# Retention, a gated product and an expert layer on one core: sums of weight quarters ordered anew, four tiles down at once in the blocks of sums, routing tile by tile

## The chip, the core and the metric

One core of a Trainium2 chip runs the program. A core has five engines, each with an instruction stream of its own that runs strictly in order: TensorE (PE in the profile; PEld is its weight load), VectorE (DVE), ScalarE (ACT), GpSimd (POOL), and SyncE (SP), which here issues most DMAs. Engines wait for one another through semaphores. The metric is device time in microseconds (us), lower is better.

## The reference

Inputs are drawn at random; 3072 tokens (4 sequences of 768) have 512 features. Three layers follow one another:

```
state = gamma * state + k v^T ; y = scale * q state          # per head, 64x64 state
a = x @ w_a ; b = x @ w_b ; x2 = (a * b) @ w_out             # 512 -> 1536 -> 512
e = argmax(x2 @ w_gate) ; out = p_e * sigmoid(x2 @ w_output_gate)[e] * relu(x2 @ w1[e]) @ w2[e]
```

The expert layer has 8 experts; each token goes to one of them. Every large product is made of three matmuls (`mm3`): high by high, high by low, low by high, of numbers split into a rounded part and a rest.

## The kernel before, in words

Tokens run in four blocks, of 512, 512, 1024 and 1024. A tile is 128 tokens; a block of 1024 has eight. The index f runs over 12 groups of 128 of the 1536 middle features; each f needs a slice of `w_a`, `w_b` and `w_out`.

**Blocks 0 and 1** are done plainly: per f two projections (`proj`, 12 matmuls each), the gate, and `down` for four tiles (12 matmuls). Block 0 also decodes the weights. Between its products, block 1 runs four other lines of work: the attention of block 2 (`attention_steps`), the routing of block 0's tiles, the weight sums (`sum_steps`), and the preparation of block 2's inputs (`x_steps`).

**The weight sums.** Blocks 2 and 3 use a scheme of seven products of quarters in place of eight; it needs four sums of quarters of each weight slice. `sum_steps` has three steps for each f: load the slice (`wsum<-wab_d`, SP), four adds on POOL (L626), split on ACT and DVE (L631, L632) and store to `q_d` on SP (L633). They stand one f after another: load, adds, split and store, then the next f's load.

**Blocks 2 and 3** (`block_of_sums`): per f seven products of 6 matmuls each into three PSUM banks (p0, p1, acc3), adds of them on DVE, and `down` for three tiles (`NOW = 3`) of the f before. The gated values of the other five tiles are kept (`later`) and go down in deferred passes over all f: block 2 has one of five tiles, block 3 one of three ("3a") and one of two ("3b"). A deferred pass loads `w_out` slices again (`load_wo`, two ahead), splits them (ACT L545, POOL L546) and splits the kept values (`gd`, ACT L746, DVE L747).

**Routing.** Tiles 0 to 15 route on DVE: per tile eight ops of two inputs each (`junkd`, L367), one for each expert's column of `w_gate`, then some fifteen small ones, a gather of the chosen column of the second gate (POOL, L376) and its use (L398), and a scatter of the token's row into a table (POOL, L355). They go in groups of up to five tiles, two columns at a time; the columns are loaded for each group (`wcol`). Tiles 16 to 23 route on PE. The first expert starts on tokens whose routing is done: `TAIL` tells how many tokens at the end are left out of its first two gathers.

What sets the order of all this is the order of calls in Python: `spread` runs the steps of the lines at the calls of `slot()`, evenly between a first and a last slot given for each line. Each engine then keeps that order.

Of the kernel before, what the change touches and what calls it, by code (L numbers as in the profile page):

```python
# [7 lines left out]
F32 = mybir.dt.float32  # L8
# [8 lines left out]
T = B * S  # L17
# [21 lines left out]
NOW = 3  # L39
LATER = 640  # L40
TAIL = 640

NDVE = 16

ROUTE_FROM = [0, 4, 4, 0]
# [4 lines left out]
Q_POOL, V_POOL = {1, 2, 3, 4, 5, 6, 7}, {1, 2, 3, 4, 5, 6, 7}  # L50
# [6 lines left out]
def attention_moe_moe2(ctx: ExitStack, tc: tile.TileContext, a: dict, out: bass.AP):  # L57
# [241 lines left out]
    def route_steps(i):  # L299
# [11 lines left out]
        def s_l():  # L311
# [12 lines left out]
            oh = p2.tile([128, 8], BF16, tag="oh", name="oh")  # L324
# [37 lines left out]
        def s_d(wc, e0):  # L362
            if e0 == 0:
                st["lg"] = p1.tile([128, 8], F32, tag=f"lg{i % 5}", name="lg")
            for e in range(2):
                junk = lp(1).tile([128, 512], BF16, tag="junkd", name="junkd")
                dve.scalar_tensor_tensor(junk, x2t[i], 1.0, wc[:, e], op0=ALU.mult, op1=ALU.mult, accum_out=st["lg"][:, e0 + e : e0 + e + 1])  # L367

        def s_m():
# [15 lines left out]
            oh = p2.tile([128, 8], BF16, tag="oh", name="oh")  # L385
# [9 lines left out]
        def s_o():  # L395
            og = p2.tile([128, 1], F32, tag="og", name="og")
            junk = lp(1).tile([128, 512], BF16, tag="junkd", name="junkd")
            dve.scalar_tensor_tensor(junk, x2t.pop(i), 1.0, st.pop("wx"), op0=ALU.mult, op1=ALU.mult, accum_out=og)  # L398
# [9 lines left out]
        if i < NDVE:  # L408
            return [s_d, s_m, s_o, s_r]
        return [s_t, s_l, s_r]  # L410

    def route_order(rs):
        plain = [st for r in rs if len(r) == 3 for st in r]
        rs = [r for r in rs if len(r) > 3]
        if not rs:
            return plain
        out = []
        for e0 in range(0, E, 2):
            w = []

            def s_w(w=w, e0=e0):
                w.append(lp(2).tile([128, 2, 512], F32, tag="wraw", name="wcol"))
                sync.dma_start(w[0].rearrange("p e n -> p (e n)"), bass.AP(a["wgt"].tensor, a["wgt"].offset + e0 * DM, [[0, 128], [1, 2 * DM]]))

            cols.append(s_w)
            for r in rs:
                out.append(lambda r=r, w=w, e0=e0: r[0](w[0], e0))
            out.append(next_cols)
        next_cols()
        next_cols()  # L430
        out += [rs[0][1], lambda: None]
        for t, r in enumerate(rs):
            if t + 1 < len(rs):
                out += [lambda r=r, n=rs[t + 1]: (r[2](), n[1]()), r[3]]
            else:
                out += [r[2], r[3]]
        return out + plain

    cols = []

    def next_cols():
        if cols:
            cols.pop(0)()

# [86 lines left out]
    passes = [(j, f) for j in (1, 2, "2d", 3, "3a", "3b") for f in range(NF1)]  # L531
# [63 lines left out]
    def evac_x2(tok0, tiles, on_dve=()):  # L595
        for t in tiles:
            x2 = lp(6).tile([128, 512], F32, tag="x2", name="x2")
            if t in on_dve:
                dve.tensor_copy(x2, accs[t])
            else:  # L600
                act.copy(x2, accs[t])
            r0 = tok0 + 128 * t
            x2t[r0 // 128] = x2
            sync.dma_start(x2_d[r0 : r0 + 128, :], x2)
# [11 lines left out]
    def sum_steps(f, pair):  # L616
        st = {}

        def s_load():
            st["w"] = room(pair[0], [128, 8, 256], F32, "wsum")  # L620
            sync.dma_start(st["w"][:, :4].rearrange("p (a q) n -> p a (q n)", a=2), wab_d[f])

        def s_add():
            w = st["w"]
            for out, x, y, op in ((5, 2, 3, ALU.add), (4, 5, 0, ALU.subtract), (6, 0, 2, ALU.subtract), (7, 1, 4, ALU.subtract)):
                pool.tensor_tensor(w[:, out], w[:, x], w[:, y], op=op)  # L626

        def s_split():
            w = st.pop("w")[:, 4:]
            t = room(pair[1], [128, 4, 2, 256], F32R, "qsum")  # L630
            act.copy(t[:, :, 0], w)  # L631
# [676 lines left out]
```

## Time and profile before

| | us |
|---|---|
| three runs | 1161.74, 1163.3 (median), 1164.52 |
| profiled execution | 1167.32 |
| its span | 1165.6 |
| PE busy in it | 1022.1 (88%) |
| DVE busy | 642.7 (55%) |
| ACT, POOL busy | 407.8, 329.8 |

The span is from the first to the last instruction. The profiled execution is some 4 us above the median, so a change is best counted as a difference. The mean granted clock of TensorE was 0.931 of its higher level. Block 1 lies between about 142 and 359 us of the span, block 2 between 359 and 526, its deferred pass up to 598.4, block 3 up to 755.5, its two passes up to 845; the rest is the experts.

### The profile page before, as it was taken

Reading aid. Unit: us, or ns where it says so; the run is one execution under the profiler, and the core shown is the slowest. Engines: PE = TensorE matmul, PEld = TensorE weight load, DVE = VectorE, ACT = ScalarE, POOL = GpSimd, SP = SyncE. Lnnn points to the kernel's source line nnn. Section 1 sums busy time; section 2 is a strip of 40 time slices with the busy share of each in tenths; the row PEclk is TensorE's granted clock in tenths of the full one; section 3 lists DMA queues with packets and bytes.
Section 4 is the critical chain, followed back from the end, with each engine's and each line's share of the span. In section 5 each row is a group of like instructions: output and inputs, shape, how many; then the busy total and the mean of one; then the engine's idle time right before and its main releaser. Section 6 shows DMA issues by size and latency. Waiting matters only on the chain.

```text
span 1165.6 us, 19944 instructions
## 1 busy us (share of the span) xinstructions
PE 1022.1 (88%) x7287; PEld 828.2 (71%) x7288; DVE 642.7 (55%) x1444; ACT 407.8 (35%) x792; POOL 329.8 (28%) x299
## 2 busy tenths in 40 slices
PE   7999997765468999997869999877799999999997
PEld 5788885544346777775647877655589998888886
DVE  5899765353355665647945654444536544444551
ACT  3667622111123222223421222244435444334441
POOL 3221044444343111243431213344212122112211
PEclk8899998786688999998898999998799999999999
DMA  6999677566647666444274656434326555345530
GB/s 250 333 327 310 222 267 240 194 213 226 205 166 256 215 223 235 170 101 162 64 219 170 205 174 176 140 127 145 100 54 203 179 177 167 123 148 180 179 108 26
DMA packets 74520, 214.99 MB, mean 184 GB/s; under 512 B 12925, under 2 KB 22397, under 8 KB 69760
## 3 DMA queue, kind: packets, MB, share of 16 engines
q1 hardware_dynamic: 67104, 193.72, 50.1%
q0 software_dynamic: 6704, 18.93, 5.2%
q8 instruction: 82, 1.34, 0.5%
q10 hardware_dynamic: 576, 0.56, 0.1%
q14 instruction: 54, 0.44, 0.1%
HBM read 169.08 MB, written 45.01 MB: 184 GB/s over the span
## 4 chain that ended last, share of the span: by engine, by line
PE 64%; DMA 12%; DVE 8%; POOL 4%; ACT 4%; issue 4%; another core or an unknown queue 2%; SPq 1%; POOLq 0%; ACTq 0%; DVEq 0%
PE p L113 9%; PE p L114 8%; PE p L115 8%; PE acc L115 8%; PE acc L113 8%; PE acc L114 8%; DMA wsum<-wab_d 5%; PE ph L114 3%; PE ph L115 3%; PE ph L113 3%; POOL wsum L626 3%; DMA wo<-wo_d 2%; DVE junkd L367 1%; DVE qsum L632 1%
## 5 line engine op out<-in xcount | busy, mean ns | idle before, releaser
L546 POOL TENSOR_TENSOR wos<-wo,wos 128x512 fp32r<-128x512 f32 x67 | 92.6, 1383 | 301.0 <-issue 170.9
L881 DVE TENSOR_TENSOR ew<-wraw,ew 128x512 fp32r<-128x512 f32 x112 | 77.0, 691 | 57.3 <-ACT ew L880 57.0
L367 DVE SCALAR_TENSOR_TENSOR junkd<-x,wcol 128x512 bf16<-128x512 f32 x128 | 102.3, 799 | 8.8 <-DMA wcol<-in_wgt 6.0
L113 PE MATMUL ph<-xe,ew 128*128 128x384 f32 (+4 forms) x288 | 98.3, 341 | 0.0
L114 PE MATMUL ph<-xe,ew 128*128 128x384 f32 (+4 forms) x288 | 95.8, 333 | 0.0
L115 PE MATMUL ph<-xe,ew 128*128 128x384 f32 (+4 forms) x288 | 95.8, 333 | 0.0
L847 DVE SCALAR_TENSOR_TENSOR hs<-ph,hs 128x384 fp32r<-128x384 f32 (+4 forms) x72 | 39.1, 543 | 101.1 <-ACT hs L846 101.0
L867 POOL DMA_INDIRECT out<-y,idx x27 | 27.4, 1016 | 228.2 <-ACT y L866 152.1
L113 PE MATMUL p<-xs,ar 128*128 128x512 f32 x192 | 83.9, 437 | 7.4 <-DVE g_sb L571 4.7
L880 ACT CAST ew<-wraw 128x512 fp32r<-128x512 f32 x112 | 68.7, 616 | 58.3 <-PE acc L115 51.5
L113 PE MATMUL p<-U,unit 128*128 128x512 f32 x192 | 79.3, 413 | 10.0 <-DVE b L725 3.9
L113 PE MATMUL acc<-ew,hs 128*128 128x512 f32 (+1 forms) x216 | 85.1, 394 | 0.6 <-ACT hs L846 0.6
L114 PE MATMUL acc<-ew,hs 128*128 128x512 f32 (+1 forms) x216 | 85.0, 393 | 0.0
L115 PE MATMUL acc<-ew,hs 128*128 128x512 f32 (+1 forms) x216 | 84.5, 391 | 0.0
L114 PE MATMUL p<-xs,ar 128*128 128x512 f32 x192 | 80.2, 418 | 0.0
L115 PE MATMUL p<-xs,ar 128*128 128x512 f32 x192 | 79.7, 415 | 0.1
L846 ACT ACTIVATE hs<-ph 128x384 fp32r<-128x384 f32 (+4 forms) x72 | 34.5, 479 | 118.2 <-PE ph L115 114.8
L115 PE MATMUL p<-U,unit 128*128 128x512 f32 x192 | 75.5, 393 | 0.0
L114 PE MATMUL p<-U,unit 128*128 128x512 f32 x192 | 75.5, 393 | 0.0
L113 PE MATMUL acc<-wos,gs 128*128 128x512 f32 x168 | 69.7, 415 | 4.0 <-ACT gs L576 4.0
L545 ACT CAST wos<-wo 128x512 fp32r<-128x512 f32 x72 | 44.5, 618 | 80.9 <-PE acc L115 69.0
L115 PE MATMUL acc<-wos,gs 128*128 128x512 f32 x168 | 68.0, 405 | 1.2 <-DVE gs L579 1.2
(213 smaller groups left out, 2408.7 us busy)
## 6 DMA issues: line engine op xcount, KB each, us to landing
wraw<-in_ex SPq DMA_DIRECT2D x64, 512.0 KB, 3.7
unit<-q_d SPq DMA_DIRECT2D x24, 1024.0 KB, 5.1
wo<-wo_d SPq DMA_DIRECT2D x72, 256.0 KB, 4.1
unit<-q_d SPq DMA_DIRECT2D x24, 768.0 KB, 4.7
wide<-in_w_ab SPq DMA_DIRECT2D x24, 512.0 KB, 5.0
q_d<-qsum SPq DMA_DIRECT2D x12, 1024.0 KB, 4.8
qk<-in_qk SPq DMA_DIRECT2D x23, 512.0 KB, 6.5
vk<-in_vk SPq DMA_DIRECT2D x23, 512.0 KB, 6.4
```

Of the source, the lines that this page charges most:

```text
L113: pe.matmul(outp, lhsT=wh, rhs=rh, start=start, stop=False, skip_group_check=more)
L114: pe.matmul(outp, lhsT=wh, rhs=rl, start=False, stop=False, skip_group_check=more)
L115: pe.matmul(outp, lhsT=wl, rhs=rh, start=False, stop=stop, skip_group_check=more)
L367: dve.scalar_tensor_tensor(junk, x2t[i], 1.0, wc[:, e], op0=ALU.mult, op1=ALU.mult, accum_out=st["lg"][:, e0 + e : e0 + e + 1])
L545: act.copy(w[:, 0], t)
L546: (eng or pool).tensor_tensor(w[:, 1], t, f32(w[:, 0]), op=ALU.subtract)
L626: pool.tensor_tensor(w[:, out], w[:, x], w[:, y], op=op)
L846: act.activation(h[:, 0, :n], p[:, :n], AF.Relu)
L847: dve.scalar_tensor_tensor(h[:, 1, :n], p[:, :n], 0.0, f32(h[:, 0, :n]), op0=ALU.max, op1=ALU.subtract)
L867: st = pool.indirect_dma_start(out=out[:, :], out_offset=bass.IndirectOffsetOnAxis(ap=ix[:, 1:2], axis=0), in_=y, in_offset=None, bounds_c ...
L880: act.copy(ew[f][:, part, 0], t[:, part])
L881: dve.tensor_tensor(ew[f][:, part, 1], t[:, part], f32(ew[f][:, part, 0]), op=ALU.subtract)
```

## The change

- `sum_steps` becomes one line for all f: two loads are issued at its start, and the order is then: adds of f+1, store of f with load of f+2, split of f+1. The store's place on SP is behind the next adds.
- `block_of_sums` has two banks for products (p1, p0) and takes four tiles down at once; acc3 is a tile's bank. The order of the products and of `down` changes, and there are seven slots in each f (before: three, of which each could hold several steps).
- One deferred pass of four tiles for each of blocks 2 and 3 (before 5, and 3 and 2). `load_wo` goes over five rounds of 12 slices in place of six.
- Routing goes by tile: tiles 0 and 1 on PE in block 1, tiles 2 to 15 on DVE in blocks 2 and 3, with all eight columns loaded once (`load_cols`), and the tile itself read back from memory (`x2r`). Tiles 16 to 19 route on PE in the last pass, 20 to 23 at the first expert (before: 22 and 23). `TAIL` is 1024.
- The six early loads of the first expert's weights all stand in the one last pass; two of their low parts go to POOL. `V_POOL` keeps only three chunks, so the `vd` product of block 2's attention is on DVE.

```diff
-NOW = 3
-LATER = 640
-TAIL = 640
-NDVE = 16
+TAIL = 1024
+ON_DVE = range(2, 16)
-Q_POOL, V_POOL = {1, 2, 3, 4, 5, 6, 7}, {1, 2, 3, 4, 5, 6, 7}
+Q_POOL, V_POOL = {1, 2, 3, 4, 5, 6, 7}, {1, 2, 3}
...
+        steps = [lambda: s_load(0), lambda: (s_load(1), s_add(0)), lambda: s_split(0)]
+        for f in range(NF1):
+            if f + 1 < NF1:
+                steps.append(lambda f=f: s_add(f + 1))
+            steps.append(lambda f=f: (s_store(f), f + 2 < NF1 and s_load(f + 2)))
+            if f + 1 < NF1:
+                steps.append(lambda f=f: s_split(f + 1))
+        return steps
...
-            ba, bb, bc = sum_bank("p0"), sum_bank("p1"), sum_bank("acc3")
-            product(bc, u, 1, "B21", True)
+            r, q = sum_bank("p1"), sum_bank("p0")
+            product(r, u, 1, "B21", True)
             a1 = p1.tile([128, 512], F32, tag="a_sb", name="a1")
-            act.copy(a1, bc)
-            product(ba, u, 0, "B11", True)
-            dve.tensor_tensor(a1, a1, ba, op=ALU.add)
-            slot()
+            act.copy(a1, r)
+            slot()
+            if f:
+                down(j, f - 1, [0])
+            product(q, u, 0, "B11", True)
+            dve.tensor_tensor(a1, a1, q, op=ALU.add)
+            slot()
...
+                down(j, f - 1, [2, 3])
                 wos.pop((j, f - 1))
             split_wo(j, f, 1)
+            product(q, u, 2, "U4", False)
+            dve.tensor_tensor(a1, a1, q, op=ALU.mult)
             gs = p2.tile([128, 2, 512], F32R, tag="gs", name="gs")
+            act.copy(gs[:, 0], a1)
+            dve.tensor_tensor(gs[:, 1], a1, f32(gs[:, 0]), op=ALU.subtract)
...
-            lines = [(attention_steps(j + 1), 0, 30), (route, ROUTE_FROM[j], 33)]
+            lines = [(attention_steps(j + 1), 0, 30)]
             if j:
-                quarters = [sum_steps(f, ((0, 1), (2, 3))[f % 2]) for f in range(NF1)]
-                lines.append(([s for q in quarters for s in q], 10, 29))
                 x_first, x_rest = x_steps(2)
-                lines += [(x_first, 26, 30), (x_rest, 30, 36)]
+                lines += [(on_pe([0, 1]), 4, 16), (sum_steps(), 9, 30), (x_first, 27, 31), (x_rest, 30, 36)]
...
-        later_pass(2, "2d", [(4, "acc3"), (3, "p1"), (5, "acc0"), (6, "acc1"), (7, "acc2")], slot, between)
+        later_pass(2, slot, lambda: between(2, 1024))
...
+        first = lambda: (load_idx0(0), gather(0, 0, T - TAIL), gather(0, 1, T - TAIL))
+        slot, flush = spread([([], 0, 1), ([*on_dve(range(8, 16)), fill_gap, first], 2, 82)])
+        block_of_sums(3, slot)
...
-        later_pass(3, "3a", [(3, "p1"), (4, "acc3"), (5, "p0")], slot, between)
-        later_pass(3, "3b", [(6, "acc0"), (7, "acc1")], slot, eng=lambda f: dve if f % 2 else pool)
+        later_pass(3, slot, lambda: between(3, 2048), lambda f: dve if f % 4 == 3 else pool)
```

The order on SP in block 1, before, about the third and fourth f of the sums (`wsum` is a slice that is loaded for the sums, `qsum` the split sums that are stored, `ar` the weights of the plain blocks, whose quarters are stored too):

```order
L633 DMA q_d<-qsum 128x2048
L621 DMA wsum<-wab_d 128x1024
L633 DMA q_d<-qsum 128x2048
L621 DMA wsum<-wab_d 128x1024
L537 DMA wo<-wo_d 128x512
L613 DMA q_d<-ar 128x2x256 x2
L614 DMA q_d<-ar 128x2x256
L138 DMA qk<-in_qk 128x1024
L141 DMA vk<-in_vk 128x1024
```

The same engine after, from the first loads on:

```order
L622 DMA wsum<-wab_d 128x1024 x2
L133 DMA qk<-in_qk 128x1024
L136 DMA vk<-in_vk 128x1024
L634 DMA q_d<-qsum 128x2048
L622 DMA wsum<-wab_d 128x1024
L537 DMA wo<-wo_d 128x512
L614 DMA q_d<-ar 128x2x256 x2
L615 DMA q_d<-ar 128x2x256
```

Two slices are loaded before the first store; from there each store is still followed by a load, but that load is for the f after next.

On DVE in one f of block 3, before (`a`, `b` and `later` are sums of products, `p` a PSUM bank, `gs` the low part for `down`):

```order
L712 TENSOR_TENSOR a_6296<-a_6296,p_6287 128x512
L367 SCALAR_TENSOR_TENSOR junkd,lg<-x_5916,wcol 128x512 x2
L367 SCALAR_TENSOR_TENSOR junkd,lg<-x_5913,wcol 128x512 x2
L725 TENSOR_TENSOR b_6315<-b_6315,p_6287 128x512
L731 TENSOR_TENSOR later<-later,p_6288 128x512
L735 TENSOR_TENSOR a_6296<-a_6296,p_6287 128x384
L736 TENSOR_TENSOR later<-a_6296,p_6287 128x128
L739 TENSOR_TENSOR gs<-a_6296,gs 128x384
```

And after, where two routing columns stand ahead of this piece:

```order
L721 TENSOR_TENSOR a_6290<-a_6290,p_6283 128x512
L365 SCALAR_TENSOR_TENSOR junkd,lg<-x2r,wcol 128x512
L344 TENSOR_TENSOR ohsum<-ohsum,oh 128x8
...
L365 SCALAR_TENSOR_TENSOR junkd,lg<-x2r,wcol 128x512 x2
L735 TENSOR_TENSOR later<-later,p_6282 128x512
L370 MAX mx<-lg 128x8
...
L738 TENSOR_TENSOR b_6313<-b_6313,p_6283 128x512
L365 SCALAR_TENSOR_TENSOR junkd,lg<-x2r,wcol 128x512
L746 TENSOR_TENSOR a_6290<-a_6290,p_6283 128x512
L749 TENSOR_TENSOR gs<-a_6290,gs 128x512
```

Routing steps now stand between any two of the adds that PE's banks wait for, one or two at a time, and the last two ops are 512 wide.

On POOL at the end of block 3, after (`xg` is the first expert's gather of tokens, `wos` the low part of a `w_out` slice; before, the two gathers stood inside pass 3a):

```order
L374 DMA wx<-in_wog,ix 128x512
L350 DMA tab_d<-pay,si 24576x4
L814 DMA xg<-x_d,idx 128x512 x2
L739 TENSOR_TENSOR later<-later,b_7027 128x512
L546 TENSOR_TENSOR wos<-wo,wos 128x512 x4
```

The two gathers, which need the table, now stand ahead of the first `w_out` slices of the last pass.

## Rows read from the trace of the kernel before

**Rows 1.** Windows by stage; window, length, busy (and instructions) per engine, clock, DMA share, GB/s.

```profile
58.30:116.60 58.30, 58.30 (x548) 47.33 (x548) 54.55 (x95) 41.13 (x76) 11.80 (x9) 1.00 0.96 318
...
142.00:359.00 217.00, 145.68 (x1466) 113.95 (x1464) 105.41 (x234) 48.31 (x88) 96.11 (x94) 0.81 0.63 217
359.00:526.00 167.00, 163.69 (x1571) 128.59 (x1571) 96.64 (x268) 42.93 (x92) 40.57 (x33) 0.99 0.59 198
526.00:598.40 72.40, 52.75 (x195) 39.77 (x195) 55.45 (x110) 24.28 (x44) 29.60 (x19) 0.88 0.40 124
598.40:755.50 157.10, 147.03 (x613) 115.06 (x613) 80.80 (x231) 38.17 (x79) 42.37 (x36) 0.97 0.57 185
755.50:845.00 89.50, 68.80 (x285) 50.17 (x286) 42.67 (x135) 38.52 (x90) 33.21 (x27) 0.86 0.39 121
845.00:877.00 32.00, 30.39 (x201) 27.23 (x201) 11.74 (x47) 9.99 (x25) 5.08 (x6) 0.95 0.25 69
```

**Rows 2.** The chain that ended last, in block 1; start, length, what.

```profile
211.27 6.44 DMA wsum<-wab_d
217.78 0.74 POOL wsum L626
...
220.76 1.05 ACT qsum L631
...
223.47 5.83 DMA wsum<-wab_d
```

**Rows 3.** Timeline of PE in block 1; start, length, instruction.

```profile
144.72 0.39 PE L115 MATMUL p<-xs,ar 128*128 128x512 f32 x1
...
146.13 0.50 PE L113 MATMUL p<-xs,ar 128*128 128x512 f32 x1
```

**Rows 4.** DMA of block 1 (142 to 359 us).

```profile
DMA packets 19299, 47.10 MB, mean 217 GB/s; under 512 B 1776, under 2 KB 10992, under 8 KB 17491
```

**Rows 5.** Timeline in block 3 about the end of the last product of one f.

```profile
676.94 0.39 PE L115 MATMUL p<-U,unit 128*128 128x512 f32 x1
...
677.37 0.56 DVE L735 TENSOR_TENSOR a<-a,p 128x384 f32<-128x384 f32 x1 [0.62 <-PE p L115]
...
677.96 0.51 ACT L738 CAST gs<-a 128x384 fp32r<-128x384 f32 x1 [2.73 <-DVE a L735]
...
678.50 0.56 DVE L739 TENSOR_TENSOR gs<-a,gs 128x384 fp32r<-128x384 f32 x1 [0.38 <-ACT gs L738]
...
679.89 0.39 PE L113 MATMUL p<-U,unit 128*128 128x512 f32 x1
```

**Rows 6.** Groups by line, whole run; count, busy, mean ns, idle before.

```profile
L367 DVE SCALAR_TENSOR_TENSOR junkd<-x,wcol 128x512 bf16<-128x512 f32 x128 | 102.3, 799 | 8.8 <-DMA wcol<-in_wgt 6.0
...
L398 DVE SCALAR_TENSOR_TENSOR junkd<-x,wx 128x512 bf16<-128x512 f32 x16 | 11.0, 687 | 10.1 <-DMA wx<-in_wog,ix 10.1
```

**Rows 7.** Timeline of DVE and POOL in the deferred pass of block 2.

```profile
540.27 0.69 DVE L367 SCALAR_TENSOR_TENSOR junkd<-x,wcol 128x512 bf16<-128x512 f32 x1
...
542.17 2.80 POOL L652 TENSOR_TENSOR xraw<-xraw 128x1024 f32<-128x1024 f32 x1
...
542.81 2.72 DVE L367 SCALAR_TENSOR_TENSOR junkd<-x,wcol 128x512 bf16<-128x512 f32 x1
```

**Rows 8.** The chain that ended last, in pass 3a.

```profile
775.36 1.05 ACT ew L458
...
778.35 3.71 DMA wo<-wo_d
...
783.01 1.28 POOL wos L546
...
789.96 0.96 ACT ew L458
```

**Rows 9.** The chain that ended last, at the first expert.

```profile
857.77 2.61 DMA tab_d<-pay,si
...
861.15 2.75 DMA tab_d<-pay,si
```

More of the change, by code (lines that the diff above doesn't have):

```diff
@@ L360, in s_r, with s_x, s_d @@
             )
[L362 to L367, printed above, removed]
+        def s_x():
+            x2 = lp(6).tile([128, 512], F32, tag="x2", name="x2r")
+            sync.dma_start(x2, x2_d[128 * i : 128 * i + 128, :])
+            st["x2"] = x2
+            st["lg"] = p2.tile([128, 8], F32, tag="lg8", name="lg")
+        def s_d(e):
+            junk = lp(1).tile([128, 512], BF16, tag="junkd", name="junkd")
+            dve.scalar_tensor_tensor(junk, st["x2"], 1.0, wcol[e], op0=ALU.mult, op1=ALU.mult, accum_out=st["lg"][:, e : e + 1])
         def s_m():
@@ L407, in route_steps @@
             s.bank = True
-        if i < NDVE:
-            return [s_d, s_m, s_o, s_r]
+        if i in ON_DVE:
+            return [s_x, *[lambda e=e: s_d(e) for e in range(E)], s_m, s_o, s_r]
         return [s_t, s_l, s_r]
[L412 to L416, printed above, removed]
-        out = []
[L418 to L437, printed above, removed]
@@ new lines, in on_dve @@
+    def on_dve(tiles):
+        rs = [route_steps(i) for i in tiles]
+        out, ends = [rs[0][0], lambda: None], []
+        for r, n in zip(rs, rs[1:] + [None]):
+            for e, step in enumerate(r[1:9]):
+                out.append(step)
+                if ends and e in (2, 5):
+                    out.append(ends.pop(0))
+                if n and e == 4:
+                    out.append(n[0])
+            out.append(r[9])
+            ends = r[10:]
+        return out + [lambda: None] + ends
@@ L446, in attention_moe_moe2, with on_pe @@
+    def on_pe(tiles):
+        rs = [route_steps(t) for t in tiles]
+        out = []
+        for i in range(len(rs) + 2):
+            for k in range(3):
+                if 0 <= i - k < len(rs):
+                    out.append(rs[i - k][k])
+        return out
     rawq = {}
@@ L529, in narrow @@
         n_read(n + 4)
-    passes = [(j, f) for j in (1, 2, "2d", 3, "3a", "3b") for f in range(NF1)]
+    passes = [(j, f) for j in (1, 2, "2d", 3, "3d") for f in range(NF1)]
     def load_wo(j, f, ahead=0):
@@ L676, in attention_moe_moe2 @@
     units = {}
[L677 to L678 removed]
+    UNIT_AT = [7, XH, XL]
     def load_unit(j, n):
@@ L1201, in attention_moe_moe2 @@
         hs = {}
-        todo = [route[0], route[3], route[1], route[4], route[2], route[5], count]
+        (t0, l0, r0), (t1, l1, r1), (t2, l2, r2), (t3, l3, r3) = [route_steps(i) for i in range(20, 24)]
+        todo = [t0, t1, lambda: (l0(), t2()), lambda: (l1(), t3()), l2, lambda: (l3(), r0()), r1, r2, r3, count]
         def after():
```

191 lines of the change are left out of this document (85 added, 106 removed).

## The prediction

> **What bounds the kernel now.** I read the busy times by stage first, then the chain that ended last inside the stages where TensorE (PE) idles, then timelines of single steps. By stage [rows 1], PE is the bound where its busy time fills the window: blocks 2 and 3 (163.7 of 167.0 us, 147.0 of 157.1). It is not the bound in block 1 (145.7 of 217.0, at a granted clock of 0.81, that is, part of the time at the lower of the two levels, 1.2 GHz), in the deferred pass of block 2 (52.8 of 72.4) and in passes 3a and 3b (68.8 of 89.5). PE's idle time in those three stages is 112 us; that is where a change of order can gain.
>
> In block 1 the chain is one ring of the weight sums, with nothing of PE in it [rows 2]: load 6.44 us, adds 217.78 to 220.76, split on ACT (1.05) and DVE and the store's issue up to the next load's start at 223.47, 2.7 together. One f takes 12.2 us, 12 take 146. PE's own need is less: 432 matmuls of the projections and `down` at 0.227 us (13 matmuls from 676.94 to 679.89 [rows 5]) are 98 us. An attention part between two products costs 1.41 - 0.23 = 1.18 us [rows 3]; with two such parts for each of 8 batches (the second taken equal), 19 us. So PE needs 117.
>
> **Block 1 after.** The wcol loads go, the sums change order, two tiles route on PE (some 4 us, an estimate: about 30 matmuls no wider than 128, at half of the 0.227 us above or a little more). PE: 121 us over 36 slots, 3.4 each. The sums stand in slots 9 to 30, so for PE 71 us. Their own ring now has two f in flight: load 6.2 (mean of the two in rows 2), adds 3.0, split and store's issue 2.7, with what lies between 12.2 us for two f, 73 us for 12. The third candidate is the DMA. Block 1 moved 47.1 MB [rows 4]; less four wcol loads of 0.52 MB, 45. Of these the sums are 12 loads of 0.52 and 12 stores of 1.05 MB, 18.9 MB; three unit loads and four stores of x2 at the end 3.9; the other 22.2 go with PE's slots, 21/36 of them beside the sums, 13. So 31.9 MB must pass in the stretch of the sums. The highest sustained rate in this trace is 318 GB/s at a DMA share of 0.96 (the first of [rows 1]), which makes 100 us: the latest of the three. Block 1 is then 9 slots (31) + 100 + 6 slots (20) + 5 for the preparation of block 2 that DVE still has to finish = 156 us, against 217: -61. Ends: PE alone, 121 + 5 = 126 (-91); a ring that stays at 9.5 us for one f because its loads queue behind stores and attention, 31 + 114 + 25 = 170 (-47), or, if it is no faster at all, 0.
>
> The Trainium skill (DMA: Bandwidth & Descriptors, Specifications) gives about 358 GB/s as a core's HBM limit, where the row has 318 at a share of 0.96; by it the stretch would be 89 us and block 1 145. I keep the row, since stores of 1 KB pieces are in the mix.
>
> **Blocks 2 and 3.** Each f has 54 matmuls in place of 51: 12 x 54 x 0.227 = 147 us for a block, 8.2 more than before; the same 8 leave the deferred passes. What else is new is the order. The gated values of f - 1 are needed for tile 0 right behind the first product of f, 6 matmuls after the last product; before, three more products lay between. From the end of that product's last matmul the chain to the low part was 677.33 to 679.06 [rows 5], 1.73 us at 384 columns; with the three ops 512/384 as long (1.63 to 2.17), 2.3 us. PE reaches the matmul that needs it after 8 x 0.227 = 1.8. So 0.5 to 0.6 us of waiting in each f, 7 a block, that the before had covered.
>
> PE also waits for DVE at four of the seven products. DVE has, per f of block 3, five adds of some 0.7 (as a 512-wide op alone takes [rows 7]), 3.5 us, and 8/12 of a tile's routing: eight columns at 0.8 [rows 6], and for the small ops and the second gate an estimate of 3 us, 9.4 us a tile, 6.3 per f. That is 9.8 of some 13.3 us of PE, with about one routing step between two adds, so most adds are still in time. I count nothing for them beyond what block 3 lost already (157.1 - 139 of matmuls = 18), which holds waits for the gather of the second gate too (10.1 us in the whole run [rows 6]). Block 2 routes six tiles in place of four, beside the attention. Both blocks: 8 + 7 = +15 each, +30. Ends: +8 each if the chain to the low part is hidden; the upper one is the third rival below.
>
> **The deferred passes.** A `w_out` slice passes through two buffers: split on ACT (0.6, a bit over half of the 1.05 for twice the width [rows 2]) and POOL 1.28, load 3.7 [rows 8], and some 1.2 of issue, 6.8 us for two f, 3.4 for one; four tiles cost PE 12 x 0.227 = 2.7. So the ring is the bound, and fewer tiles do not help, but fewer passes do. Block 2's pass: 12 x 3.4 = 41, the last `down` 2.7, start 4: 48 against 72.4, where DVE's routing stood in the way (PE 52.8 busy). -24; ends -31 (PE bound, 12 x 2.7 + 9) and -8, if the preparation of block 3 on POOL and DVE keeps it at 64.
>
> Block 3's pass has six loads of expert weights, one every two f. Such a load cost, from its ACT copy to POOL's `wos`, 775.36 to 784.29 = 8.9 us [rows 8], of a period of 14.6 for four f (775.36 to 789.96), because SP waits with the next `w_out` load until the split has freed the expert buffer. At one every two f, 8.9 us for two: 53 for 12. At its start POOL stands in the first expert's gathers, which need the table of tile 15: scatter landed, index load, two gathers, then `wos`, some 11 us after the scatter's issue, of which products and `down` cover 6 to 7: 4.5 us. With the last `down` 2.7: 60 against 89.5, -29.5. Ends -40 and -15.
>
> **The first expert's stage.** Four scatters in place of two, one after another, 861.15 - 857.77 = 3.4 us apart [rows 9]: 6.8 later; PE has two more tiles to route there, so part is covered: +6, ends 0 and +10. The experts themselves are as before.
>
> **Sum.** -61 + 30 - 24 - 29.5 + 6 = -78.5 us. The profiled execution took 1167.3 us (span 1165.6), 4.0 above the median of the runs; the difference is set against the median: 1163.3 - 78.5 = 1084.8, so 1085.
>
> **Rivals.** *PE alone decides.* The sums overlap better than the row's 318 GB/s lets expect, and the low part comes in time: block 1 140 (-77), blocks +8 and +5, passes -26 and -37, expert +3: -124, 1039. For it speaks that every wait named above is short; against it, that the DMA was at 0.96 wherever the trace asked that much of it. Chance 0.18.
>
> *The sums stay a chain.* Loads still stand behind stores on one queue, and ACT, which holds the split, also copies PE's banks: at 10.5 us for one f, block 1 is 31 + 126 + 25 = 182 (-35): 1111. That is the change not doing what it says, in part. Against it: the order shows two loads ahead of the first store. Chance 0.14.
>
> *POOL holds DVE in the blocks.* A routing column takes 0.69 us alone and 2.72 when POOL's 2.80 us op runs [rows 7]. Per f POOL has two ops of 1.3; if each falls on such a column and its wait reaches PE, 2.0 us an f: 24 x 2.0 = +48, 1133. For it: more columns stand between the adds than before; against: adds with one input in PSUM kept 0.69. Chance 0.12. The Trainium skill states the rule behind it (GPSIMD Engine Reference, Specifications): SBUF access is shared with VectorE, with contention for instructions with two SBUF inputs; rows 7 agree.
>
> *Slower than before.* The same two-bank blocks, but with every add late: the gather of the second gate holds DVE, its adds and so both banks. It decides from 78.5/24 = 3.3 us an f beyond the 13.4 counted, that is, when DVE's in-order work reaches 16.7 us an f: 9.8 + 2.6 (POOL) leaves 4.3, a full wait of 6 us for each of the 14 tiles' gathers and as much again. At 4 us an f: 1181. Chance 0.04. No change within 0.2% (about what a measurement of this kernel can tell from none): 0.02.
>
> **How the numbers follow.** The forecast, 1062 to 1108 by the ends of its terms taken partly together, has 0.50; the rivals have 0.18, 0.14, 0.12, 0.04, and no change 0.02. The range for 8 in 10 is 1042 to 1122: it leaves out half of the first rival and most of the third and what is beyond. Faster: 0.50 + 0.18 + 0.14 + 0.12 = 0.94; same 0.02; slower 0.04.
>
> **What would show it.** Block 1 of some 156 us with a DMA share near 0.9, and a chain with two loads of the sums in flight; if its share stays at 0.6 and the chain still reads load, adds, split, load, the second rival is right. In the blocks, a wait of about 0.5 us of PE for `gs` at tile 0 of each f, and PE busy above 90%; a wait for the adds (`b`, `a`) with long `junkd` beside POOL means the third. One pass of 48 and one of 60 us. I am wrong in the main if block 1 takes over 185 us, or if blocks 2 and 3 grow by over 25 us each.

## The result, and the profile after

The changed kernel takes 1073.9 us (median of 4 runs, 1070.7 to 1076.0) against 1163.3, a ratio of 0.923 [0.9205, 0.9256]. On another chip, in a later series, it took 1081.7 against 1165.7, 0.927 [0.9251, 0.9295]. The predicted time was 1085, with a range of 1042 to 1122.

The profiled execution took 1076.0 us (span 1074.3) where that of before took 1167.3, 91.3 us less. Stage by stage, cut at PE's first instruction of each stage:

| stage | before, us | after, us | change | predicted |
|---|---|---|---|---|
| block 1 | 217.0 | 150.3 | -66.7 | -61 |
| block 2 | 167.0 | 180.2 | +13.2 | +15 |
| pass of block 2 | 72.2 | 43.1 | -29.1 | -24 |
| block 3 | 157.1 | 167.1 | +10.0 | +15 |
| last pass(es) | 89.7 | 58.4 | -31.3 | -29.5 |
| first expert | 29.8 | 42.5 | +12.7 | +6 |
| experts | 290.5 | 290.9 | +0.4 | 0 |

What is left, -0.5, lies ahead of block 1. The windows of the kernel after answer to [rows 1]; the columns are the same: the window, its length, busy time (and instructions) of PE, PEld, DVE, ACT and POOL, granted clock, DMA share, GB/s.

```profile
141.70:292.10 150.40, 130.81 (x1486) 102.81 (x1486) 83.42 (x146) 47.13 (x83) 81.48 (x80) 0.94 0.85 292
292.10:471.50 179.40, 173.25 (x1609) 132.12 (x1607) 113.82 (x317) 45.65 (x99) 46.13 (x37) 1.00 0.60 202
471.50:515.30 43.80, 39.16 (x156) 29.71 (x157) 32.27 (x24) 22.64 (x36) 28.41 (x15) 0.96 0.33 101
515.30:681.50 166.20, 156.26 (x654) 119.20 (x652) 101.02 (x310) 39.40 (x85) 48.62 (x39) 0.98 0.55 178
681.50:740.70 59.20, 49.31 (x224) 36.88 (x224) 35.65 (x84) 27.53 (x57) 22.73 (x17) 0.94 0.40 135
740.70:783.30 42.60, 32.49 (x214) 28.30 (x214) 14.34 (x77) 9.73 (x32) 7.07 (x8) 0.92 0.26 62
```

PE's idle time in block 1 fell from 71 to 20 us, and in the deferred passes from 40 to 14.5. The DMA share of block 1 rose from 0.63 to 0.85. The mean granted clock of block 1 rose with it, from 0.81 to 0.94, and PE's busy time there fell by 15 us, with 20 more matmuls.

Where [rows 2] showed one load, its adds, its split, its store and only then the next load, the timeline of the kernel after (start, length, instruction) reads:

```profile
208.23 3.65 POOL L626 TENSOR_TENSOR wsum<-wsum 128x256 f32<-128x256 f32 x4 [1.61 <-DMA wsum<-wab_d]
208.63 0.33 SPq L634 DMA_DIRECT2D q_d<-qsum  x1
209.05 0.38 SPq L622 DMA_DIRECT2D wsum<-wab_d  x1
...
220.37 2.92 POOL L626 TENSOR_TENSOR wsum<-wsum 128x256 f32<-128x256 f32 x4 [4.59 <-DMA wsum<-wab_d]
```

The store of one f and the load of the next but one are issued while POOL adds the f between. At 220.37 POOL had still stood 4.59 us for a load that was issued at 209.05, 11.3 us earlier: the loads are now on their way in time, and slow (7.7 us from issue to landing in the median, 5.7 before).

The moved bytes answer to [rows 4] (47.10 MB), and the windows of 15 us in the stretch of the sums show the rate:

```profile
DMA packets 18314, 43.91 MB, mean 292 GB/s; under 512 B 1584, under 2 KB 10800, under 8 KB 16506
```

```profile
190.00:205.00 15.00, 14.09 (x174) 10.94 (x174) 10.27 (x21) 3.71 (x7) 12.39 (x13) 0.92 1.02 308
...
220.00:235.00 15.00, 7.59 (x91) 5.49 (x89) 4.31 (x7) 4.25 (x7) 7.56 (x11) 0.95 0.81 307
...
250.00:265.00 15.00, 14.40 (x180) 11.50 (x179) 7.33 (x14) 4.92 (x8) 10.41 (x11) 1.00 1.01 367
```

In blocks 2 and 3, the wait for the low part of the gated values that was forecast from [rows 5] is there. The timeline of block 3 after the change, about tile 0 of one f:

```profile
586.55 0.62 ACT L748 CAST gs<-a 128x512 fp32r<-128x512 f32 x1 [1.36 <-DVE a L746]
...
586.78 0.39 PE L110 MATMUL p<-B,unit 128*128 128x512 f32 x1
...
587.20 0.69 DVE L749 TENSOR_TENSOR gs<-a,gs 128x512 fp32r<-128x512 f32 x1 [0.69 <-ACT gs L748]
587.22 0.19 PEld L108 LDWEIGHTS acc<-wos,gs 128*128 128x128 f32 x1 [0.47 <-ACT gs L748]
...
587.95 0.19 PEld L110 LDWEIGHTS acc<-wos,gs 128*128 128x128 f32 x1 [0.43 <-DVE gs L749]
...
588.29 0.40 PE L108 MATMUL p<-B,unit 128*128 128x512 f32 x1
```

From the last matmul of the first product (586.78) to the next product (588.29) it is 1.51 us; four matmuls at 0.227 would be 0.91. So 0.6 us is lost in this f. Measured in the same way in the trace, ten of the eleven f of block 3 lose 0.44 to 0.96 us each, 6.0 in all, and nine of block 2 lose 0 to 1.2 us, 5.5 in all (the others have another instruction of PE in between, or a record missing).

The first expert's stage is where the forecast was short. Waits of PE there (total, times, longest), and the chain that ended last:

```profile
PE pg L836 <- DMA xg<-x_d,idx: 7.2, 1, 7.2
```

```profile
765.58 0.96 DMA tab_d<-pay,si
...
768.92 2.72 DMA tab_d<-pay,si
771.66 2.23 DMA idx<-tab_d
...
774.69 3.39 DMA xg<-x_d,idx
```

As in [rows 9], each scatter starts behind the landing of the one before, by 0.8 us here; the last lands at 771.6, then the indices are read and the rows gathered, and PE stands 7.2 us for them.

### The profile page after: what moved, and what is told of

Its sections match the earlier page's. It is cut to its first block, busy times and chain, and to the rows that moved or that the text cites. A ratio compares the mean times of both kernels' runs of the same rounds, so it can differ in the third digit from the quotient of the medians.

```text
span 1074.3 us, 19807 instructions
## 1 busy us (share of the span) xinstructions
PE 995.1 (93%) x7314; PEld 802.6 (75%) x7315; DVE 633.0 (59%) x1383; ACT 398.7 (37%) x768; POOL 318.2 (30%) x282
## 5 line engine op out<-in xcount | busy, mean ns | idle before, releaser
L546 POOL TENSOR_TENSOR wos<-wo,wos 128x512 fp32r<-128x512 f32 x58 | 84.2, 1452 | 95.1 <-ACT wos L545 39.6
L108 PE MATMUL acc<-wos,gs 128*128 128x512 f32 x192 | 81.3, 424 | 4.7 <-ACT gs L576 3.8
L108 PE MATMUL p<-xs,ar 128*128 128x512 f32 x192 | 78.7, 410 | 5.2 <-DVE g_sb L571 2.8
L365 DVE SCALAR_TENSOR_TENSOR junkd<-x2r,wcol 128x512 bf16<-128x512 f32 x112 | 76.7, 685 | 10.3 <-DMA x2r<-x_d 9.4
L110 PE MATMUL acc<-wos,gs 128*128 128x512 f32 x192 | 78.5, 409 | 2.3 <-DVE gs L749 1.6
L109 PE MATMUL acc<-wos,gs 128*128 128x512 f32 x192 | 77.1, 402 | 0.0
L110 PE MATMUL p<-xs,ar 128*128 128x512 f32 x192 | 75.8, 395 | 0.3
L109 PE MATMUL p<-xs,ar 128*128 128x512 f32 x192 | 75.5, 393 | 0.0
```

Source lines behind the costliest of these rows:

```text
L108: pe.matmul(outp, lhsT=wh, rhs=rh, start=start, stop=False, skip_group_check=more)
L109: pe.matmul(outp, lhsT=wh, rhs=rl, start=False, stop=False, skip_group_check=more)
L110: pe.matmul(outp, lhsT=wl, rhs=rh, start=False, stop=stop, skip_group_check=more)
L365: dve.scalar_tensor_tensor(junk, st["x2"], 1.0, wcol[e], op0=ALU.mult, op1=ALU.mult, accum_out=st["lg"][:, e : e + 1])
L546: (eng or pool).tensor_tensor(w[:, 1], t, f32(w[:, 0]), op=ALU.subtract)
```

## The experiments

Differences of a few us are read from the stage of the profile that an edit touches, since the experts' stage, which no edit touches, is 291 to 300 us long from one chip to another. Ratios are to the kernel before on the same chip.

**The old order of the sums in the new kernel.** Each f has its three steps by itself again, with the store in the last of them.

```diff
-        steps = [lambda: s_load(0), lambda: (s_load(1), s_add(0)), ...]
+        return [s_load, s_add, s_split]
...
-                lines += [..., (sum_steps(), 9, 30), ...]
+                lines += [..., ([s for q in quarters for s in q], 9, 30), ...]
```

> The changed kernel with the weight sums put back in their old order (load, adds, split and store of one f, then the next f), all else as changed. Theory (the ring of load, adds and split bounded block 1, and two f in flight removed it): block 1 returns from 150 us to 200 to 217, the whole to 1125 to 1140 us. Rival (block 1 became shorter because its routing on VectorE, with the gathers it waits for, and 2 MB of column loads left it): block 1 grows by under 15 us, the whole stays under 1090 us.

Measured: 1141.0 us, ratio 0.976 [0.9732, 0.9786]. Its window of block 1:

```profile
142.20:351.70 209.50, 144.98 (x1485) 113.80 (x1485) 79.39 (x147) 47.27 (x84) 73.42 (x80) 0.84 0.64 210
```

With the old ring, block 1 is 209.5 us, the DMA share back at 0.64 and the clock at 0.84: the other edits in block 1 (no `wcol` loads, two tiles routed on PE) are worth 7.5 us of the 66.7. The order of the sums is the cause of the rest, 59 us with those edits in place.

**The new order of the sums alone.** The kernel before, with `sum_steps` of the change and nothing else.

```diff
-        return [s_load, s_add, s_split]
+        steps = [lambda: s_load(0), lambda: (s_load(1), s_add(0)), ...]
...
-                lines.append(([s for q in quarters for s in q], 10, 29))
+                lines.append((sum_steps(), 9, 30))
```

> The kernel before with the new order of the weight sums alone. Theory: block 1 falls from 217 us to 155 to 165 (DMA share near 0.85 to 0.95, with the column loads still in it), the whole to 1100 to 1112 us. Rival (routing on VectorE in block 1 holds it as well): block 1 stays above 180 us, the whole above 1125 us.

Measured: 1115.1 us, ratio 0.954 [0.9499, 0.9576]; time and block 1 lie just above the ranges of the theory.

```profile
141.80:307.60 165.80, 133.03 (x1466) 104.35 (x1464) 113.16 (x234) 48.19 (x88) 101.57 (x94) 0.91 0.82 284
```

Block 1 falls to 165.8; blocks 2 and 3 and the passes stay where they were (165.9, 154.3, 70.9 and 91.5 us). So block 1 gives 51 us by this one edit, and the time falls by 54 of some 90 (ratios 0.954 and 0.923). It moves 284 GB/s x 165.8 us = 47.1 MB, the whole kernel 43.9: the last 15 us of block 1 come with 3.2 MB less to move, some 10 us at the rates seen here, and with less of DVE's work (113 against 83 us busy).

**Less for the DMA beside the sums.** The quarters' stores (three a slice, 9.4 MB in all) go earlier, ahead of the sums where they can.

```diff
+KEEP_AT = {0: [0, 1, 2], 1: [3, 4, 5], 2: [6, 7], 3: [8], 5: [9], 7: [10], 9: [11]}
-                    keep_quarters(f)
+                    for g in KEEP_AT.get(f, []):
+                        keep_quarters(g)
```

> The changed kernel with the stores of the plain blocks' weight quarters (0.79 MB per f) moved up: eight f of them in the first three f of block 1, where the DMA engines have room, the rest spread behind. Same bytes in all. Theory (the stretch of the sums is bound by the DMA engines, share 0.97 to 1.05 there): 2 to 3 MB less in it, at some 0.33 MB per us, so block 1 is 6 to 10 us shorter, ratio to the changed kernel 0.991 to 0.995. Rival (the ring's latency or TensorE bounds it): no difference beyond 2 us.

Measured: 1081.6 us, ratio 0.926 [0.9234, 0.9287]. Block 1 is 148.2 us, 2 less; 6 to 10 were expected. The time as a whole shows no gain: the changed kernel's ratio was 0.923 and 0.927.

```profile
141.80:174.00 32.20, 32.15 (x440) 25.76 (x439) 14.95 (x37) 8.99 (x20) 9.08 (x10) 1.00 1.01 339
174.00:205.00 31.00, 26.63 (x352) 20.69 (x352) 17.59 (x47) 9.49 (x21) 20.88 (x22) 1.00 0.76 260
...
265.00:280.00 15.00, 14.46 (x60) 11.03 (x60) 13.34 (x12) 6.26 (x10) 8.17 (x6) 1.00 0.65 244
```

The stores did move: the DMA is full from 142 to 174, and no longer at 174 to 205 and 265 to 280. Yet the sums end only 2.5 us sooner (last store at 270.0 against 272.5). So the DMA is not the only thing that holds them: what else stands close behind it is the question of the next three runs.

**More for the DMA beside the sums.** Twelve copies of 0.52 MB in block 1 whose data nothing uses.

```diff
         def s_add(f):
+            act.dma_start(more_d[f], wab_d[f])
```

> The changed kernel, with twelve DMAs more in block 1: beside each step of the sums' adds ACT issues a copy of one 0.52 MB piece from memory to memory, which nothing waits for; it is read and written, 6.3 MB each way. Theory (block 1 of the changed kernel is bound by the DMA, with a share of 0.85 in the mean and 0.81 to 1.05 in the stretch of the sums): at the 330 GB/s of that stretch block 1 grows by 19 us if a byte copied counts once, 38 us if it counts twice. Rival (the DMA has slack, since POOL's order, the ring and TensorE's slots pace the sums): under 8 us.

Measured: 1097.4 us, ratio 0.941 [0.9372, 0.9446], against 0.927 for the changed kernel; block 1 is 165.9 us, 15 longer than the 150.3 and 151.1 of its two profiles, and no stage but the experts' moved by more than 2. The copies' DMA queue in block 1 (packets, MB, share of 16 engines' time), and the window with the highest rate:

```profile
q10 hardware_dynamic: 384, 6.29, 10.0%
```

```profile
250.00:265.00 15.00, 14.15 (x139) 11.15 (x133) 5.41 (x11) 3.75 (x6) 8.45 (x10) 0.91 1.03 376
```

The copies' packets took 10.0% of 165.9 us, 16.6 us of the engines' time, and block 1 grew by 15: nearly all of it is paid, with a byte copied counted once. The loads and stores of the sums landed later, too (8.2 and 8.5 us in place of 7.7 and 7.5), which for a ring with two f in flight would be some 9 us. And the copies are not quite free of everything else: SP's waits from 160 to 300 us (total, times, longest) name their landing:

```profile
SPq L636 <- DMA more_d<-wab_d: 4.9, 2, 3.8
SPq L615 <- DMA more_d<-wab_d: 3.1, 1, 3.1
```

So bytes added in block 1 are paid nearly in full, as a stage bound by the DMA would have it. The run leaves open how much of the 15 us is the DMA's own time, how much comes through the longer ring, and how much through the queue that issues the loads.

**The wait that PE shows in block 1.** In the changed kernel PE stands longest for the attention's decayed queries (`qd`), which POOL makes in order with the adds of the sums. The run takes the three small edits together (the run "all three" below) and moves `qd` to DVE.

```diff
-Q_POOL, V_POOL = {1, 2, 3, 4, 5, 6, 7}, {1, 2, 3}
+Q_POOL, V_POOL = {1, 2, 3}, {1, 2, 3}
```

> The combined kernel, and in block 1 the decayed queries of the attention (one op of 2.3 us on GpSimd for each of eight batches) run on VectorE (about 0.7 us each), as the decayed values already do; nothing is left out. Theory (GpSimd works in order, a batch's queries stand behind adds of the sums that wait for a load, and TensorE stood 5.5 us for them in the combined kernel, 7.7 in the changed one): the wait goes, block 1 shrinks from 148.4 to 142 to 145 us, the kernel by 3 to 6 us. Rival (VectorE works in order too, and the queries then stand behind a split that waits; or the load that the adds wait for is what ends last anyway): block 1 within 1.5 us of 148.4.

Measured: 1072.3 us, ratio 0.920 [0.9167, 0.9224]; block 1 149.8 us, against 148.4. The theory is out. PE's waits in block 1 of the changed kernel, and then of this one:

```profile
PE sc L209 <- POOL qd L149: 8.5, 2, 7.7
```

```profile
PE sc L210 <- issue: 6.2, 2, 5.7
```

The queries' op is off POOL, and PE stands 5.7 us at the same line, one batch later (5.5 in the kernel it starts from). The list of waits names no cause, but the timeline of this run does:

```profile
245.74 2.90 POOL L627 TENSOR_TENSOR wsum<-wsum 128x256 f32<-128x256 f32 x4 [5.65 <-DMA wsum<-wab_d]
...
249.75 1.23 DVE L632 TENSOR_TENSOR qsum<-wsum,qsum 128x1024 fp32r<-128x1024 f32 x1 [8.32 <-ACT qsum L631]
...
251.56 0.69 DVE L150 TENSOR_TENSOR qd<-qk,dec 128x512 f32<-128x512 f32 x1
...
252.34 0.71 PE L210 MATMUL sc<-qd,qk 64*64 64x64 f32 x16 [5.69 <-issue]
```

PE starts 0.1 us after `qd` ends. On DVE `qd` now stands behind the sums' split, which stood 8.3 us for the split on ACT, as that did for POOL's adds, and those 5.65 us for a load. That is the rival put on record: the queries stand behind a split that waits, and the load of the sums is what is late. The wait was where lateness showed, not what made it.

**An earlier start of the sums.** The kernel of the run before, with the sums two slots earlier.

```diff
-                lines += [..., (sum_steps(), 9, 30), ...]
+                lines += [..., (sum_steps(), 7, 30), ...]
```

> The kernel of the run before it (queries on VectorE), and the sums' steps are spread over slots 7 to 30 of block 1 in place of 9 to 30, so the first load starts two slots, some 7 us, earlier. Theory (the stretch of the sums has its own length by its loads, adds and stores, 97 us in the changed kernel from the first load to the last store, so that an earlier start is an earlier end): block 1 shrinks by 4 to 7 us against the run before it. Rival (the end is set by the bytes of the whole block or by TensorE's slots): under 2 us.

Measured: 1078.8 us, ratio 0.925 [0.9214, 0.9286], 6 us more than the run before it by the medians, though its six runs spread from 1071.6 to 1084.3; block 1 is 155.0 us. The first load is issued at 172.3 in place of 177.4 and the last store at 277.9 in place of 272.7: in the two profiles, an earlier start brought a later end. Of the two theories neither had this sign. The longest waits of SP, which issues in order, from 160 to 285 us (total, times, longest), first in the run with `qd` on DVE, then in this one:

```profile
SPq L635 <- DVE qsum L632: 34.0, 8, 8.7
SPq L538 <- POOL wos L547: 31.1, 9, 6.7
```

```profile
SPq L538 <- POOL wos L547: 41.0, 8, 10.8
SPq L635 <- DVE qsum L632: 11.6, 4, 6.6
```

The sum of all of SP's waits hardly changed (79 and 82 us): the time that the sums' stores no longer wait for their split, SP now waits for buffers: for the `w_out` slice that POOL must still split, behind its adds, and for the queries' buffer (12.1 us in place of 5.7). While it stands there, no load of the sums behind it is issued: from 205 to 220 us the DMA share is 0.65 in this run and 1.04 in the run before it. Together with the stores moved earlier this points to a second bound of block 1: one in-order queue that issues nearly everything. No run takes that queue by itself, so it is argued, not shown.

**Tile 0 later.** In blocks 2 and 3, tile 0 of f - 1 goes down behind the second product of f, not the first.

```diff
-            if f:
-                down(j, f - 1, [0])
             product(q, u, 0, "B11", True)
             dve.tensor_tensor(a1, a1, q, op=ALU.add)
             slot()
+            if f:
+                down(j, f - 1, [0])
```

> The changed kernel with tile 0 going down behind the second product of an f instead of the first, in blocks 2 and 3. Theory (TensorE waits some 0.6 us for the low part of the gated values in each f): the gap goes, 22 x 0.6 = 13 us less, blocks 2 and 3 each 6 to 7 us shorter. Rival (the wait then shows at the next product, since VectorE's chain is what is late): under 4 us less in all.

Measured: 1080.2 us, ratio 0.925 [0.9221, 0.9271], not to be told from the changed kernel's as a whole. In the profile block 2 is 176.8 us (-3.4) and block 3 164.6 (-2.5); the wait at tile 0 is gone: from the last matmul of the product before it to the next product it is 0.92 us, where it was 1.51.

```profile
583.40 0.39 PE L110 MATMUL p<-B,unit 128*128 128x512 f32 x1
...
584.32 0.39 PE L108 MATMUL p<-U,unit 128*128 128x512 f32 x1
```

So the mechanism was right, and the wait itself was nearly as long as forecast, 5.5 and 6.0 us in the two blocks; but taking it away gives back only about half of it. The rest is lost elsewhere, as the rival said in part: in block 3, PE now stands 0.9 and 0.5 us for ACT's `b` and `a` (none before) and 0.7 us longer for DVE's `ohsum`. How far one profile can be trusted here: with this edit, alone or with others, block 2 takes 176.8 to 178.8 us in four profiles and block 3 163.8 to 164.6; in the six profiles with both blocks as in the changed kernel they take 180.2 to 180.9 and 164.3 to 167.1.

**POOL's product on DVE.** It tests the rival in which POOL holds DVE.

```diff
-            pool.tensor_tensor(g2, g2, b2, op=ALU.mult)
+            dve.tensor_tensor(g2, g2, b2, op=ALU.mult)
```

> The changed kernel, but in the blocks of sums the product of the deferred tiles' gate (one 512-wide op an f) runs on VectorE in place of GpSimd; nothing is left out. Theory (VectorE's adds come in time but for some 3 to 5 us a block, and GpSimd's op beside them costs little: the columns of the routing took 685 ns on average in the changed kernel): one op of 0.7 us more on VectorE an f, blocks of 180 and 166 us within 2 us or up to 3 us longer. Rival (the third of the prediction's, GpSimd's op holds VectorE for 2 us where the two meet, and the adds come late for it): the blocks become 0.5 to 1 us an f faster, 6 to 12 us each.

Measured: 1079.3 us, ratio 0.925 [0.9217, 0.9291]; blocks 181.8 and 165.7 us, 347.5 together against 347.3. For this op the rival is out. Why the op costs nothing in either place is seen in the changed kernel's timeline of DVE and POOL:

```profile
596.39 0.67 DVE L738 TENSOR_TENSOR b<-b,p 128x512 f32<-128x512 f32 x1
...
596.99 0.68 DVE L365 SCALAR_TENSOR_TENSOR junkd<-x2r,wcol 128x512 bf16<-128x512 f32 x1
597.20 1.64 POOL L739 TENSOR_TENSOR later<-later,b 128x512 f32<-128x512 f32 x1
```

POOL's product waits for DVE's add (L738); by the time POOL starts, DVE is already in its next op. Here it is POOL that takes longer (1.64 us, 1.27 to 1.32 alone), and DVE's column keeps its 0.68. All eleven columns of `w_gate` that met this product had begun before it, and took 0.68 to 0.69 us. The Trainium skill (SBUF — State Buffer, Who interferes with whom) states that a VectorE instruction with two inputs in SBUF contends with a GpSimd instruction that reads SBUF, and that the order of issue, not the shape of the op, decides which of them blocks. The rows agree.

**The last pass in two.** The last pass's four tiles as two passes of two, with as many matmuls; what stood between their steps is parted over the two, or put ahead of the first.

```diff
-        later_pass(3, slot, lambda: between(3, 2048), ...)
+        later_pass(3, slot, None, ..., range(2))
+        later_pass(3, slot, None, ..., range(2, 4), "3e")
```

> The changed kernel, but the last deferred pass of four tiles done as two passes of two tiles each, one after the other: the matmuls and the routing steps are the same in number, the output weights are loaded 24 times in place of 12. Theory (a deferred pass is paced by its weights: one load and split per 128 rows of weights, some 4 to 5 us whatever the number of tiles that use it, as 89.7 us over the 24 steps of the two passes before, 3.7 us each): the last passes take 85 to 95 us in place of 58.4, the kernel 25 to 35 us longer than the changed one. Rival (a pass is paced by TensorE, so 48 products take the same in one pass or in two): the stage grows by one pass's filling, 3 to 6 us, and the kernel by as much.

Measured: 1107.3 us, ratio 0.949 [0.9464, 0.9524]; the stage is 80.4 us against 59.1 for the changed kernel on the same chip, +21, and the kernel is 25.6 us longer. The stage lies between the two theories, nearer to the first, and the kernel's time within the first. Its window:

```profile
686.30:766.80 80.50, 60.62 (x213) 41.24 (x214) 42.80 (x97) 38.51 (x77) 34.87 (x25) 0.80 0.41 129
```

A step of two tiles takes 80.4/24 = 3.35 us, one of four 59.1/12 = 4.9. Neither "3.4 us whatever the tiles" (that is right for two tiles, not for four beside the expert loads) nor PE alone. PE idles 20 us in place of 10 and is 11 us longer busy with 11 fewer recorded instructions, at a granted clock of 0.80 in place of 0.94: half of the price is PE waiting, by the profile for split weights (19 us in place of 8), the other half its longer busy time at the lower mean clock that came with the waits.

**The scatters earlier.** The routing steps of the last four tiles drawn together.

```diff
-todo = [t0, t1, lambda: (l0(), t2()), lambda: (l1(), t3()), l2, lambda: (l3(), r0()), r1, r2, r3, count]
+todo = [t0, lambda: (l0(), t1()), lambda: (l1(), t2()), lambda: (r0(), l2(), t3()), lambda: (r1(), l3()), r2, r3, count]
```

> The changed kernel, but in the first expert's stage the routing steps of the last four tiles are drawn together, so that the first of their payloads is ready about two matmul slots earlier; nothing is left out. Theory (the stage waits at the end of a chain in series: six scatters of 2.6 to 3.5 us each behind the other's landing, the load of the indices, then the gather, and TensorE stood 7.2 us for that gather): the last four scatters start 3 to 5 us earlier, the stage shrinks from 42.5 to 37 to 40 us, the kernel by 2 to 5 us. Rival (the stage is long because VectorE and TensorE share the logits' small steps, and drawing them together only moves the wait to the logits): the stage stays within 1.5 us of 42.5 and the time within 0.15%.

Measured: 1077.9 us, ratio 0.924 [0.9219, 0.9261]; the stage is 40.8 us against 42.7 on the same chip, where 37 to 40 was expected. PE's wait for the gather is 5.9 us in place of 7.4:

```profile
PE pg L836 <- DMA xg<-x_d,idx: 5.9, 1, 5.9
```

The chain in series holds the stage, as the theory had it, but only 2 us could be taken from it in this way, because the scatters of the last tiles still follow one another.

**All three.** Earlier stores, tile 0 later and the scatters earlier in one kernel.

> The changed kernel with three edits at once: the quarters' stores issued earlier in block 1 (2 us in its own run), tile 0 of the down products moved behind the second product (3.4 and 2.5 us in its own run) and the routing steps of the last four tiles drawn together. Theory (the three lie in different stages and add up): 6 to 11 us less than the changed kernel, ratio to the kernel before 0.914 to 0.919. Rival (what one stage gains, the next gives back, because the chain of the weights and the gathers runs across stages): within 3 us of the changed kernel, ratio 0.921 to 0.925.

Measured: 1071.1 us (5 runs, 1068.0 to 1072.8), ratio 0.918 [0.9161, 0.9206]; the changed kernel on the same chip 1081.7, ratio 0.927:

> The changed kernel once more, on the chip of the next three, so that small differences are taken on one chip. Both theories expect the ratio measured before, 0.923, within 0.003, block 1 at about 150 us, the blocks of sums at about 180 and 167 us, and the first expert's stage at about 42 us of profiled time.

That ratio is 0.004 above the first, a little more than was expected; the stages came out as expected. The three edits take 10.6 us or 1% off the changed kernel, and give the lowest ratio here; the run with `qd` on DVE, which holds them too, can't be told from it (0.920).

Against the changed kernel's profile on the same chip, block 1 is 2.7 us shorter, blocks 2 and 3 3.4 and 2.6, the last pass 2.3 and the first expert 3.0. The edits add up, as the theory had it; the 2.3 us of the last pass belong to none of them, and show how far one profile can differ from the next.

## Why the prediction was right, and where it was not

**Block 1: -61 forecast, -66.7 measured.** The chain of [rows 2] was the bound before, and its two orders alone make 209.5 or 150.3 us. The step that named the DMA as the latest of three candidates (100 us for 31.9 MB at 318 GB/s) is near in each of its numbers: from the first load to the last store it is 96.8 us, 31.3 MB, 323 GB/s. The same stretch in the changed kernel, with the quarters' stores earlier, and with the added copies:

```profile
175.70:272.50 96.80, 82.46 (x970) 65.33 (x960) 50.98 (x96) 29.55 (x51) 61.37 (x66) 0.95 0.94 323
```

```profile
175.90:270.00 94.10, 83.41 (x966) 65.85 (x956) 48.87 (x95) 29.72 (x51) 62.29 (x66) 0.95 0.90 308
```

```profile
177.70:289.70 112.00, 87.98 (x971) 68.45 (x960) 47.64 (x96) 29.44 (x51) 58.29 (x66) 0.89 0.95 336
```

With 6.4 MB more the stretch is 15.2 us longer; with 2.3 MB less, which is 7 us at 323 GB/s, only 2.7 us shorter, and the share falls. So the DMA is not the only bound, and the close match of the 100 us is in part luck. The figure of about 358 GB/s that the prediction cited beside the row is not the limit of this run: the Trainium skill (HBM Reference, Specifications) calls it a core's share with both cores of a pair streaming, and about 425 what a core alone reaches, bounded by its DMA engines. One core runs here, and 376 over 15 us in the run with added copies is above the share; none of the windows of that length cut here reached 425. What the step left out is that the DMA isn't full all the way (0.81 at 220 to 235). That SP, standing for buffers, is what leaves it idle there is argued above, not shown.

**Blocks 2 and 3: +15 each forecast, +13.2 and +10.0 measured.** The 8.2 us of matmuls are counted, not estimated; the wait at tile 0 was there, 5.5 and 6.0 us where 7 was forecast, in nearly every f. In block 2 the two make up the growth. Block 3 grew by less because a wait that it had before is gone: PE stood 4.5 us there for ACT's `x` (L601).

```profile
PE acc L113 <- ACT x L601: 4.5, 1, 4.5
```

What the step did not say is that a wait is worth less than its length: the run without it is only 3.4 and 2.5 us shorter.

**The passes: -24 and -29.5 forecast, -29.1 and -31.3 measured.** "Fewer tiles do not help, but fewer passes do" is right in its sign: the same products in one pass more cost 21 us. The ring of 3.4 us a step was seen with two tiles (3.35); 43.1 us for the twelve steps of block 2's pass are 3.6 each with the start and the last `down` in them, so for four tiles there the ring is at most that, and the allowance of 7 us beside it was too much.

**The first expert: +6 forecast, +12.7 measured. This is the step that failed in size.** It priced two more scatters in series at 6.8 us and took part of them as covered by PE's routing of two more tiles. Nothing was covered: PE's busy time rose by 4.3 us (28.2 in the same stage before), and the wait for the gather by 6.2 (1.0 us before, 7.2 after), since the scatters come after the tiles' routing, not beside it. The scatters say the same. The first of the last four is issued 16.9 us after the stage's start, where the first of two was 12.6 ([rows 9]), and the last one 11.2 us behind it, where it was 3.4; together that is 12 of the 12.7 us.

```profile
757.74 0.96 POOL L350 DMA_INDIRECT tab_d<-pay,si  x1 [11.38 <-DVE junk L347]
```

The rest of PE's time, some 2 us, is small waits. The other terms erred the other way, by 19 us in all, which hid it in the sum: that the total is no more than 11 us off is in part luck.

**The rivals.** *PE alone decides*: no, block 1 keeps 20 us without PE's work, and the low part does come late. *The sums stay a chain*: no; with the old order the profile looks as it said (0.64, one load at a time), with the new one not. *POOL holds DVE in the blocks*: not in the columns that it named. They answer to [rows 6] and [rows 7], in the groups by line:

```profile
L365 DVE SCALAR_TENSOR_TENSOR junkd<-x2r,wcol 128x512 bf16<-128x512 f32 x112 | 76.7, 685 | 10.3 <-DMA x2r<-x_d 9.4
```

685 ns in the mean where it was 799. The rival took the 2.72 us of one meeting for the price of every meeting, and didn't ask which of the two engines would start first. Another op did pay: three times in the two blocks DVE's `gs` began 0.5 to 0.8 us behind POOL's `wos` and took 1.32, 1.29 and 1.06 us in place of 0.69, and in those f PE lost 1.24, 1.21 and 0.96 us at tile 0 in place of some 0.6. That is under 2 us, not 48. *Slower than before* by the second gate's gather: the blocks grew by 10 and 13 us, and PE's waits for DVE's adds in them were 3.1 and 5.2 us in all.

## What to carry to other kernels

Where a stage idles on a chain of load, compute, store and load again, put the store of one item and the load of the next but one behind the compute of the item between; then look for the next bound at once, by adding traffic that nothing waits for as well as by taking some away, since with two bounds close together taking away can show next to nothing where adding shows nearly the whole price (2 us and 15 us here). A wait that the profile puts on an engine in such a stage may be a symptom: moving its op to another engine left the time as it was, because the op then stood behind a late load there too. When a change moves work past a chain in series (scatter, scatter, index load, gather), count the whole chain from the last producer, and take nothing as covered unless it runs beside it.

## What the runs showed of the hardware

- Where DVE and POOL meet with ops from SBUF, the order of their starts decides who pays. In the changed kernel's passes, ten `gd` ops of DVE that began before POOL's `wos` took 0.68 to 0.69 us, six that began after it 1.43 to 1.78. In the run with two passes one that began 0.2 us behind POOL's 1024-wide op took 2.7, as its timeline shows:

```profile
703.31 2.37 POOL L459 TENSOR_TENSOR ew<-wraw,ew 128x1024 fp32r<-128x1024 f32 x1
...
703.50 2.73 DVE L757 TENSOR_TENSOR gd<-later,gd 128x512 fp32r<-128x512 f32 x1 [1.29 <-ACT gd L756]
```

  The 2.72 us beside POOL in [rows 7] is such a meeting, with POOL's op 0.64 us ahead. DVE's adds with one input in PSUM kept 0.67 to 0.69 beside POOL's `wos` (20 of `a<-a,p`).
- A full DMA share is not one rate: in block 1 of the changed kernel, two windows of 15 us at shares of 1.02 and 1.01 moved 308 and 367 GB/s, and one in the run with the added copies 376 at 1.03. Which part of the traffic makes the difference was not taken apart.
- Earlier issue on an in-order queue can end later: in one profile of each kernel, 5 us earlier at the first load, 5 us later at the last store.
